# Loading v in two transfers a batch, reordering K's columns on their way out of PSUM, and setting the order of all work by a list scheduler inside a windowed-attention and adapter kernel

## The chip, the cores and the metric

The kernel runs on one core of a Trainium2 chip. The metric is the device time of one execution in microseconds, lower is better. A core has five engines that run their own instruction streams and wait for each other by semaphores: PE (TensorE, matrix products, with weight loads shown as PEld), DVE (VectorE), ACT (ScalarE), POOL (GpSimd) and SP (SyncE). Here POOL issues all loads, because they convert from float32 to float16 on the way, and SP issues all stores. Both run on the same DMA engines.

## The reference

Eight batches of eight heads, 576 positions, head size 64. Each position attends to positions at most 32 away. The result, laid out as 4608 rows of 512, goes through a mixture of eight adapters of rank 16, two per row, and is added to itself.

```python
scores = scale * np.matmul(q, k.transpose(0, 1, 3, 2))
mask = np.abs(pos[:, None] - pos[None, :]) <= window      # window = 32
scores = np.where(mask, scores, -1000000000.0)
attn = softmax(scores)
x = (attn @ v).transpose(0, 2, 1, 3).reshape(B * S, H * D)
logits = x @ w_gate                                       # 8 experts, the best 2 kept
w = softmax(the 2 kept logits)
out = x + sum over the 2 experts of w * ((x @ A[e]) @ B[e])
```

## The kernel before

Heads are taken in pairs (the index o is the half, n the pair within the batch, four pairs a batch), so that a unit u = 4b + n is one pair of one batch, 32 units in all. A unit has nine key blocks of 64 positions; eight consecutive blocks, of one unit or two, make a score tile, and there are 36 of them. The stages:

- **Loads.** `load` (line 85) brings q or k of a batch in three transfers of 96 partitions. `load_v` (93) brings v of a batch in eight transfers, two halves times four, each to 8 partitions, in rows of two positions. They land in one of three buffers `vbd`. `shift_v` (103) then copies, for each half, the second position of each row into 32 partitions further down, on DVE.
- **q and k to columns.** `regroup` (111) puts a tile of 96 rows into transposable order on DVE. `transposes` (181) does eight transposes for q and eight for k on PE into a PSUM tile of the pool `pt` (two buffers). q goes to `qT` by one ACT copy (192). k goes to `kT` in two copies of 64 partitions, the first half on DVE (204), the second on ACT (206). Within a block of 64 the k columns stand in the order (j, f), which is the order in which the eight v transfers place the positions.
- **Scores.** `score` (208): two matmuls write the mask into a PSUM tile of the pool `pw` (three buffers), eight add q times k, and one ACT instruction (222) takes the exponential into one of four `PT` buffers.
- **Values.** `pv` (226): 13 matmuls (238) with v and a column of ones, then a reciprocal (246) and a multiplication (247) on DVE into x.
- **Adapters**, once a batch, in four steps (`moe_step`, 325): five groups of four transposes of x (258), each with its DVE copy (261); 20 matmuls for router and first factor (269); the gate, twelve small DVE instructions and one on ACT (279 to 293); transposes back (302) and an ACT copy (305); output products (313, and 316 which adds x itself), in PSUM two groups at a time, an ACT copy (319) and stores on SP (323).

The order of work is written out by hand. Before the loop, the loads of batches 0 and 1 are issued on POOL, DVE clears the buffers of batch 0, and POOL clears those of the other batches (lines 164 to 166, by `zero` on line 135) and then issues six weight loads (170 to 179). In the loop over u, at the first unit of a batch come the loads of the batch after next; then regroup and transposes of one tile of the next batch, the scores for the next unit, the values of this unit, and one adapter step of the previous batch. The framework adds the semaphores, and each engine works its own stream off in order. It gives each load on POOL one of eight semaphores in turn, so the ninth waits for the first to land. A pool with n buffers makes the n+1st allocation wait until the first one is free.

Of the kernel before, what the change touches and what calls it, by code (L numbers as in the profile page):

```python
# [9 lines left out]
F16 = mybir.dt.float16  # L10
# [4 lines left out]


# [5 lines left out]

@with_exitstack
def kernel(
# [11 lines left out]
    B, H, S, D = q.shape  # L41
    assert (B, H, S, D) == (8, 8, 576, 64)
    N, DD = out.shape
    E = moe_w_gate.shape[1]
    R = moe_A.shape[2]
    ER = E * R
    NP = H // 2
    NB = 9
    NG = 5
    TB = 8  # L50
    J = 8
    PH = S // J
    NF = NP * PH
    NT3 = 3
    FT = NF // NT3
    GS = 188
    VD = D + 1
    V0 = 8
    VW = 136
    NS = NP * NB  # L60
    NEG = -30000.0
    NU = B * NP
    NT = NU * NB // TB
    QP = 32

    const = tc.alloc_tile_pool(name="const", bufs=1)
    load_pool = tc.alloc_tile_pool(name="load", bufs=2)
    cast_pool = tc.alloc_tile_pool(name="cast", bufs=2)
    x_pool = tc.alloc_tile_pool(name="xsb", bufs=2)
    moe_pool = tc.alloc_tile_pool(name="moe", bufs=2)  # L70
    ob_pool = tc.alloc_tile_pool(name="ob", bufs=3)
    small = tc.alloc_tile_pool(name="small", bufs=3)
    pw = tc.alloc_tile_pool(name="pw", bufs=3, space=bass.MemoryType.PSUM)
    pt = tc.alloc_tile_pool(name="pt", bufs=2, space=bass.MemoryType.PSUM)

    NV = 3
    vbd = [const.tile([128, NS, 2 * VW], F16, name=f"vbd{i}") for i in range(NV)]
    qTs = [const.tile([128, QP + NP * S + QP], F16, name=f"qT{i}") for i in range(2)]
    kTs = [const.tile([128, NS, 128], F16, name=f"kT{i}") for i in range(2)]
    NPT = 4  # L80
    PTs = [const.tile([128, TB, 256], F16, name=f"PT{i}") for i in range(NPT)]

    raw, qk = {}, {}

    def load(b, w):
        d = load_pool.tile([FT, NT3, 2, J * D], F16, tag=f"l{w}", name=f"l{w}")
        src = (q, k)[w][b].rearrange("(o n) (p j) d -> (n p) o (j d)", o=2, j=J)
        for t in range(NT3):
            nc.gpsimd.dma_start(out=d[:, t], in_=src[FT * t:FT * t + FT])  # L89
        raw[b, w] = d  # L90
        qk[b, w] = cast_pool.tile([FT, NT3, J, 2, D], F16, tag=f"c{w}", name=f"c{w}")

    def load_v(b):
        d = vbd[b % NV]
        src = v[b].rearrange("(o n) (a p j two) d -> o j p (n a) (two d)",
                             o=2, p=8, j=4, two=2)
        for o in range(2):
            for j in range(4):
                p0 = 64 * o + 8 * j
                c0 = VW * o + V0  # L100
                nc.gpsimd.dma_start(out=d[p0:p0 + 8, :, c0:c0 + 2 * D], in_=src[o, j])  # L101

    def shift_v(b):
        d = vbd[b % NV]
        for o in range(2):
            p0 = 64 * o
            c0 = VW * o + V0
            nc.vector.tensor_copy(out=d[p0 + 32:p0 + 64, :, c0:c0 + D],  # L108
                                  in_=d[p0:p0 + 32, :, c0 + D:c0 + 2 * D])

    def regroup(b, t):
        for w in (0, 1):
            nc.vector.tensor_copy(  # L113
                out=qk[b, w][:, t],
                in_=raw[b, w][:, t].rearrange("p o (j d) -> p j o d", j=J))

    load(0, 0)
    load(0, 1)
    load_v(0)

    ident = const.tile([128, 128], F16)
    make_identity(nc, ident)


    maskT = const.tile([128, 2, 2, 4, 8], F16)
    nc.gpsimd.memset(maskT, 0.0)
    nc.gpsimd.affine_select(out=maskT, in_=maskT, compare_op=ALU.is_ge, fill=NEG,
                            base=0, channel_multiplier=1,
                            pattern=[[0, 2], [-1, 2], [-2, 4], [-8, 8]])
    nc.gpsimd.affine_select(out=maskT, in_=maskT, compare_op=ALU.is_ge, fill=NEG,  # L130
                            base=64, channel_multiplier=-1,
                            pattern=[[0, 2], [1, 2], [2, 4], [8, 8]])

    def zero(eng, ap):
        eng.memset(ap, 0.0)  # L135

    def init_kq(i, eng):
        zero(eng, kTs[i][0:64, :, 64:128])
        zero(eng, kTs[i][64:128, :, 0:64])
        zero(eng, qTs[i][:, 0:QP])  # L140
        zero(eng, qTs[i][:, QP + NP * S:])

    def init_v(i, eng):
        zero(eng, vbd[i][0:64, :, VW + V0 - 1:VW + V0 + D])
        zero(eng, vbd[i][64:128, :, V0 - 1:V0 + D])
        eng.memset(vbd[i][0:64, :, V0 - 1:V0], 1.0)
        eng.memset(vbd[i][64:128, :, VW + V0 - 1:VW + V0], 1.0)

    init_kq(0, nc.vector)
    zero(nc.vector, PTs[0][:, :, 0:64])  # L150
    zero(nc.vector, PTs[0][:, :, 192:256])
    zero(nc.vector, qTs[0][:, QP + S:QP + S + 32])
    for t in range(NT3):
        regroup(0, t)
    for i in range(1, NPT):
        zero(nc.vector, PTs[i][:, :, 0:64])
        zero(nc.vector, PTs[i][:, :, 192:256])
    init_v(0, nc.vector)

    load(1, 0)  # L160
    load(1, 1)
    load_v(1)
    shift_v(0)
    init_kq(1, nc.gpsimd)
    init_v(1, nc.gpsimd)
    init_v(2, nc.gpsimd)

    WA_sb = const.tile([128, 4, ER + E], F16)
    for c in range(4):
        nc.gpsimd.dma_start(  # L170
            out=WA_sb[:, c, 0:ER],
            in_=moe_A.transpose([1, 0, 2])[128 * c:128 * c + 128],
        )
    nc.gpsimd.dma_start(
        out=WA_sb[:, :, ER:],
        in_=moe_w_gate.rearrange("(c p) e -> p c e", p=128),
    )
    B_sb = const.tile([128, DD], F16)
    nc.gpsimd.dma_start(out=B_sb, in_=moe_B.rearrange("e r d -> (e r) d"))

    def transposes(b, t):
        for w in (0, 1):
            src = qk[b, w].rearrange("p t j o d -> p t j (o d)")
            tp = pt.tile([128, 1024], F16, tag="t", name="tp")
            for j in range(J):
                slot = j if w == 0 else 4 * (j % 2) + j // 2
                nc.tensor.matmul(  # L187
                    out=tp[:, FT * slot:FT * slot + FT], lhsT=src[:, t, j, :],
                    rhs=ident[0:FT, 0:FT], is_transpose=True, start=True, stop=True)
            if w == 0:  # L190
                c0 = QP + J * FT * t
                nc.scalar.copy(  # L192
                    out=qTs[b % 2][:, c0:c0 + J * FT].rearrange("p (f j) -> p f j", j=J),
                    in_=tp[:, 0:J * FT].rearrange("p (j f) -> p f j", j=J))
            else:
                kt = tp[:, 0:J * FT].rearrange("p (j a f) -> p a j f", j=J, f=8)
                a0 = NS // NT3 * t
                a1 = a0 + NS // NT3
                for o in range(2):
                    dst = kTs[b % 2][64 * o:64 * o + 64, a0:a1, 64 * o:64 * o + 64]  # L200
                    dst = dst.rearrange("p a (j f) -> p a j f", f=8)
                    src_ = kt[64 * o:64 * o + 64]
                    if o == 0:
                        nc.vector.tensor_copy(out=dst, in_=src_)  # L204
                    else:
                        nc.scalar.copy(out=dst, in_=src_)  # L206

    def score(t):
        ps = pw.tile([128, TB, 128], F32, tag="w", name="ps")
        for i in range(0, TB, 4):  # L210
            nc.tensor.matmul(out=ps[:, i:i + 4],  # L211
                             lhsT=maskT.rearrange("p o a j f -> p (o a j f)"),
                             rhs=bcast(ident, 1, 4), start=True, stop=False)
        for i in range(TB):
            u, a = divmod(TB * t + i, NB)
            b, n = divmod(u, NP)
            c0 = S * n + 64 * a
            nc.tensor.matmul(  # L218
                out=ps[:, i], lhsT=kTs[b % 2][:, NB * n + a, :],
                rhs=qTs[b % 2][:, c0:c0 + 128],  # L220
                start=False, stop=(i % 4 == 3))
        nc.scalar.activation(out=PTs[t % NPT][:, :, 64:192], in_=ps,  # L222
                             func=AF.Exp, scale=1.0 / float(D) ** 0.5)

    xs = {}

    def pv(u):
        b, n = divmod(u, NP)
        if n == 0:
            xs[b] = x_pool.tile([128, NG, DD], F16, tag="x", name="xb")  # L230
        po = pw.tile([128, 1024], F32, tag="w", name="po")
# [174 lines left out]
```

## Time and profile before

| | us |
|---|---|
| time, median of 3 runs | 226.85 |
| lowest and highest run | 225.37, 232.73 |
| the profiled execution, its own time | 226.42 |
| its span, first to last instruction | 224.3 |
| busy: PE, DVE, ACT, POOL | 142.0, 122.5, 102.4, 98.9 |
| mean granted clock of TensorE | 0.888 |

The profile is one execution. Its page lists busy time by engine, then the span in 40 slices of 5.6 us with a digit for the busy share of each (9 is 90% or more; PEclk is the granted clock in tenths), the DMA queues, and the chain of waits: from the last instruction back, at each step to what released it. Groups of instructions are shown as line, engine, operation, output <- input, shape, count, then busy us, mean ns of one, then idle time of the engine before them and what ended it. In the timeline a row is start, duration, engine, line, operation. Matmuls overlap, so a PE row's duration is longer than its share of the engine, and the distance between two starts is the better price.

### The profile page before, as it was taken

The numbers are of one execution on the slowest core, as the hardware profiler recorded it, in microseconds if no ns is written. First come the engines' busy times: TensorE is split into PE (matmuls) and PEld (weight loads), VectorE is DVE, ScalarE is ACT, GpSimd is POOL, SyncE is SP. The second block draws the span as 40 slices with busy tenths as digits, with TensorE's granted clock in tenths as the row PEclk, the third lists the DMA queues.
The fourth block names the chain that finished last, engine by engine and source line by source line (L and its number), as shares of the span: only waits on it lengthen the run. The fifth ranks groups of instructions, "written<-read, shape, count | busy, mean of one in ns | idle before, by whom it ended". The sixth has DMA issues, their size and how long they took to land.

```text
span 224.3 us, 4265 instructions
## 1 busy us (share of the span) xinstructions
PE 142.0 (63%) x1720; PEld 114.2 (51%) x1720; DVE 122.5 (55%) x305; ACT 102.4 (46%) x125; POOL 98.9 (44%) x139
## 2 busy tenths in 40 slices
PE   0071995115769584968497759774977599639470
PEld 0041973115748473747375646563756476527440
DVE  5289469315532974395525962785258616743710
ACT  2012796011448445741667258626672576026032
POOL 8899799995776756097105930730000000000000
PEclk9998599955879999796969999999699969997967
DMA  6999910999999999899925995790230023002306
GB/s 74 167 108 193 91 5 1 29 154 145 122 177 157 256 147 154 178 179 77 189 85 133 101 165 136 158 79 1 85 129 3 0 82 130 3 3 82 129 0 210
DMA packets 57970, 24.20 MB, mean 108 GB/s; under 512 B 44000, under 2 KB 53344, under 8 KB 57952
## 3 DMA queue, kind: packets, MB, share of 16 engines
q0 software_dynamic: 52704, 14.51, 85.2%
q1 hardware_dynamic: 5248, 9.44, 12.0%
q8 instruction: 13, 0.21, 0.5%
q14 instruction: 5, 0.04, 0.1%
HBM read 28.85 MB, written 9.44 MB: 171 GB/s over the span
## 4 chain that ended last, share of the span: by engine, by line
PE 33%; DVE 25%; POOL 14%; DMA 14%; issue 7%; ACT 5%; ACTq 0%; DVEq 0%; POOLq 0%
DMA l<-in_k_dram 9%; PE pz L269 5%; PE po L238 5%; PE tx L258 5%; POOL l L89 5%; PE ps L211 5%; DVE xb L247 4%; DVE vbd L108 4%; DVE c L113 4%; POOL vbd L135 4%; PE ps L218 4%; PE pd L313 4%; PE pd L316 3%; DMA vbd<-in_v_dram 3%; DVE zs L293 3%
## 5 line engine op out<-in xcount | busy, mean ns | idle before, releaser
L101 POOL DMA_DIRECT2D vbd<-in_v_dram x64 | 47.4, 747 | 40.3 <-PE po L238 30.3
L187 PE MATMUL tp<-ident,c 96*128 96x96 f16 x384 | 27.8, 228 | 29.8 <-POOL ident masks.py:199 12.8
L222 ACT ACTIVATE PT<-ps 128x1024 f16<-128x1024 f32 x36 | 36.4, 1024 | 13.9 <-PE ps L218 13.6
L187 PEld LDWEIGHTS <-c 96*128 96x128 f16 x384 | 23.3, 111 | 33.7 <-DVE c L113 19.6
L192 ACT COPY qT<-tp 128x768 f16<-128x768 f16 x24 | 19.2, 799 | 44.3 <-PE tp L187 44.3
L238 PE MATMUL po<-vbd,PT 128*128 128x130 f16 x416 | 32.3, 227 | 11.0 <-DVE vbd L108 7.2
L238 PEld LDWEIGHTS <-PT 128*128 128x128 f16 x416 | 27.1, 102 | 13.0 <-DVE vbd L108 8.1
L113 DVE COPY c<-l 96x1024 f16<-96x1024 f16 x48 | 20.3, 456 | 15.3 <-DMA l<-in_q_dram 9.3
L206 ACT COPY kT<-tp 64x768 f16<-64x768 f16 x24 | 19.0, 793 | 20.7 <-DVE kT L204 20.6
L319 ACT COPY obt<-pd 128x1024 f32<-128x1024 f32 (+1 forms) x24 | 20.8, 870 | 14.2 <-PE pd L316 11.7
L211 PE MATMUL ps<-ident,maskT 128*128 128x512 f16 x72 | 27.0, 448 | 0.2
L218 PEld LDWEIGHTS <-kT 128*128 128x128 f16 x288 | 22.5, 110 | 8.5 <-issue 3.3
L247 DVE TENSOR_TENSOR xb<-po,rc 128x640 f16<-128x640 f32 x32 | 26.3, 823 | 0.9
L218 PE MATMUL ps<-qT,kT 128*128 128x128 f16 x288 | 26.5, 242 | 0.0
L204 DVE COPY kT<-tp 64x768 f16<-64x768 f16 x24 | 13.1, 546 | 24.1 <-PE tp L187 24.1
L246 DVE RECIPROCAL rc<-po 128x10 f32<-128x10 f32 x32 | 6.8, 213 | 31.4 <-PE po L238 31.3
L258 PE MATMUL tx<-ident,xb 128*128 128x128 f16 x160 | 16.9, 235 | 9.4 <-DVE xT L261 8.7
L313 PE MATMUL pd<-B_sb,zT 128*128 128x512 f16 x40 | 16.9, 422 | 4.2 <-ACT zT L305 4.2
L258 PEld LDWEIGHTS <-xb 128*128 128x128 f16 x160 | 12.6, 106 | 12.5 <-issue 10.4
L261 DVE COPY xT<-tx 128x512 f16<-128x512 f16 x40 | 16.4, 421 | 4.3 <-PE tx L258 2.3
L302 PE MATMUL tz<-ident,zs 128*128 128x128 f16 x40 | 3.6, 221 | 22.5 <-DVE zs L293 22.5
L316 PE MATMUL pd<-ident,xT 128*128 128x128 f16 x160 | 17.8, 242 | 0.0
(47 smaller groups left out, 163.4 us busy)
## 6 DMA issues: line engine op xcount, KB each, us to landing
out_dram<-obt SPq DMA_DIRECT2D x24, 256.0 KB, 2.4
l<-in_q_dram POOLq DMA_DIRECT2D x24, 192.0 KB, 5.4
l<-in_k_dram POOLq DMA_DIRECT2D x24, 192.0 KB, 6.3
vbd<-in_v_dram POOLq DMA_DIRECT2D x64, 72.0 KB, 6.9
out_dram<-obt SPq DMA_DIRECT2D x16, 192.0 KB, 2.4
WA_sb<-in_moe_A_dram POOLq DMA_DIRECT2D x4, 32.0 KB, 3.1
B_sb<-in_moe_B_dram POOLq DMA_DIRECT2D x1, 128.0 KB, 3.1
WA_sb<-in_moe_w_gate_dram POOLq DMA_DIRECT2D x1, 8.0 KB, 2.8
```

The lines of the kernel that those rows point to most:

```text
L101: nc.gpsimd.dma_start(out=d[p0:p0 + 8, :, c0:c0 + 2 * D], in_=src[o, j])
L113: nc.vector.tensor_copy(out=qk[b, w][:, t], in_=raw[b, w][:, t].rearrange("p o (j d) -> p j o d", j=J))
L187: nc.tensor.matmul(out=tp[:, FT * slot:FT * slot + FT], lhsT=src[:, t, j, :], rhs=ident[0:FT, 0:FT], is_transpose=True, start=True, stop=True)
L211: nc.tensor.matmul(out=ps[:, i:i + 4], lhsT=maskT.rearrange("p o a j f -> p (o a j f)"), rhs=bcast(ident, 1, 4), start=True, stop=False)
L218: nc.tensor.matmul(out=ps[:, i], lhsT=kTs[b % 2][:, NB * n + a, :], rhs=qTs[b % 2][:, c0:c0 + 128], start=False, stop=(i % 4 == 3))
L222: nc.scalar.activation(out=PTs[t % NPT][:, :, 64:192], in_=ps, func=AF.Exp, scale=1.0 / float(D) ** 0.5)
L238: nc.tensor.matmul(out=po[:, GS * g:GS * g + 2 * VD], lhsT=PTs[t % NPT][:, sl, off:off + 128], rhs=rhs[:, :, V0 - 1:V0 + D], start=(i == 0 ...
L247: nc.vector.tensor_tensor(out=xs[b].rearrange("p g (h n d) -> p g h n d", h=2, n=NP)[:, :, :, n], in0=pog[:, :, :, 1:VD], in1=bcast(rc, 3, ...
L258: nc.tensor.matmul(out=tp[:, 128 * c:128 * c + 128], lhsT=xs[b][:, g, 128 * c:128 * c + 128], rhs=ident, is_transpose=True, start=True, st ...
L313: nc.tensor.matmul(out=pd[:, i], lhsT=zT[:, g], rhs=B_sb, start=True, stop=False)
L316: nc.tensor.matmul(out=pd[:, i, 128 * c:128 * c + 128], lhsT=xT[:, g, c], rhs=ident, start=False, stop=(c == 3))
L319: nc.scalar.copy(out=ob[:, 0:n], in_=pd[:, 0:n])
```

## The change

Three things, and what goes with them.

**v in two transfers.** Each half of a batch's v comes as 32 partitions at once. Partition p of a half now holds positions 2p and 2p + 1 of its block, and the shift on DVE stays as it was.

```diff
-        src = v[b].rearrange("(o n) (a p j two) d -> o j p (n a) (two d)",
-                             o=2, p=8, j=4, two=2)
-        for o in range(2):
-            for j in range(4):
-                p0 = 64 * o + 8 * j
-                c0 = VW * o + V0
-                nc.gpsimd.dma_start(out=d[p0:p0 + 8, :, c0:c0 + 2 * D], in_=src[o, j])
+    def LV(b, o):
+        src = v[b, 4 * o:4 * o + 4].rearrange("n (a p two) d -> p (n a) (two d)", p=32, two=2)
+        p0, c0 = 64 * o, VW * o + V0
+        nc.gpsimd.dma_start(out=vbd[b % NV][p0:p0 + 32, :, c0:c0 + 2 * D], in_=src)
```

**K's columns in that order.** The copy from PSUM writes the order (r, f, j) in place of (j, f), and both halves are on ACT. The mask is built for the new order.

```diff
-                kt = tp[:, 0:J * FT].rearrange("p (j a f) -> p a j f", j=J, f=8)
...
-                    if o == 0:
-                        nc.vector.tensor_copy(out=dst, in_=src_)
-                    else:
-                        nc.scalar.copy(out=dst, in_=src_)
+        kt = ps("TR", b, 1, t)[:, 0:J * FT].rearrange("p (r j a f) -> p a r f j", r=2, j=4, f=8)
+        for o in range(2):
+            dst = kTs[b % 2][64 * o:64 * o + 64, BT * t:BT * t + BT, 64 * o:64 * o + 64]
+            nc.scalar.copy(out=dst.rearrange("p a (r f j) -> p a r f j", r=2, j=4),
+                           in_=kt[64 * o:64 * o + 64])
```

**A list scheduler.** The function `tasks` describes the kernel as tasks: loads LD and LV, shift SV, regroup RG, transposes TR, the copies EQ and EK, scores SC, exponential EX, values PV, their scaling MU, and the adapter steps TX, XE, PZ, G1, GA, G2, TZ, ZE, PD, OB and stores ST. Each has an engine, a cost, its predecessors, a due time (its unit number plus an offset of its kind) and, if it writes PSUM, the kind of buffer it takes and the task that gives it back. `plan` runs them through a model of the engines: the task that can start earliest goes next, and among those ready on an engine the one with the earliest due time. The kernel then emits all instructions in that order, and the PSUM buffer of each task is the one the model gave it.

```diff
+            lim = cand[0] + (horizon if e in ("PE", "ACT", "DVE") else 0.0)
...
+                if s <= lim and (pick is None or (t.due, t.seq) < (pick[1].due, pick[1].seq)):
+                    pick = (s, t)
+            if best is None or pick[0] < best[0]:
+                best = pick
...
+    ts, order = plan()
...
+    for t in order:
+        do[t.key[0]](*t.key[1:])
+        if t.key[0] in ("LD", "LV"):
+            loads += 1
+            if loads == 4:
+                constants()
+            elif loads == 8:
+                init_v(1, nc.gpsimd)
+            elif loads == 10:
+                init_kq(1, nc.gpsimd)
+            elif loads == 16:
+                weights()
+                init_v(2, nc.gpsimd)
```

What goes with it:

- The raw tiles of q and k lie in seven buffers each, by tile, in place of two by batch, and the regrouped ones in three by tile.
- The transposes of x go in three PSUM tiles of two, two and one groups, with one DVE copy for each tile.
- The third output copy of a batch (one group) is on DVE; the first two stay on ACT.
- POOL's clearing of buffers is spread between the loads, as the last lines of the diff show; identity and mask are made after the fourth load, and the weights are loaded after the sixteenth.
- The zeroing of `vbd` starts one column earlier, at an even column.
- PSUM has three wide and two narrow buffers as before.

In the built program PE has the same 1720 matmuls as before, and the loads come in the order q, k, q, k, half of v, q, k, half of v for each batch. On ACT, three q copies, six half copies of k and two exponentials (the first ahead of the last two half copies) come ahead of anything of batch 1.

More of the change, by code (lines that the diff above doesn't have):

```diff
@@ L14 @@
 AX = mybir.AxisListType
+B, H, S, D = 8, 8, 576, 64
+E, R, DD = 8, 16, 512
+ER = E * R
+NP = H // 2
+NB = 9
+NG = 5
+TB = 8
+J = 8
+PH = S // J
+NF = NP * PH
+NT3 = 3
+FT = NF // NT3
+GS = 188
+VD = D + 1
+V0 = 8
+VW = 136
+NS = NP * NB
+BT = NS // NT3
+NEG = -30000.0
+NU = B * NP
+NT = NU * NB // TB
+QP = 32
+NV, NPT, NRAW, NCAST, NX, NXT, NOB = 3, 4, 7, 3, 2, 2, 3
+NW, NTP = 3, 2
 def bcast(ap, axis, n):
@@ L111, in regroup @@
[L111 to L129, printed above, removed]
@@ L208, in score, with many @@
-    def score(t):
-        ps = pw.tile([128, TB, 128], F32, tag="w", name="ps")
+    assert tuple(q.shape) == (B, H, S, D)
+    const = tc.alloc_tile_pool(name="const", bufs=1)
+    psum = tc.alloc_tile_pool(name="psum", bufs=1, space=bass.MemoryType.PSUM)
+    small = tc.alloc_tile_pool(name="small", bufs=3)
+    def many(n, shape, dt, name):
+        return [const.tile(shape, dt, name=f"{name}{i}") for i in range(n)]
+    vbd = many(NV, [128, NS, 2 * VW], F16, "vbd")
+    qTs = many(2, [128, QP + NP * S + QP], F16, "qT")
@@ L314, in moe_out, with PD @@
+    def PD(b, h):
+        pd = ps("PD", b, h).rearrange("p (i c) -> p i c", c=DD)
+        for i, g in enumerate(gs(h)):
+            nc.tensor.matmul(out=pd[:, i], lhsT=zTs[b % 2][:, g], rhs=B_sb,
                              start=True, stop=False)
             for c in range(4):
-                nc.tensor.matmul(out=pd[:, i, 128 * c:128 * c + 128], lhsT=xT[:, g, c],
-                                 rhs=ident, start=False, stop=(c == 3))
-        ob = ob_pool.tile([128, 2, DD], F32, tag="ob", name="obt")
@@ L319, in moe_out, with OB @@
-        nc.scalar.copy(out=ob[:, 0:n], in_=pd[:, 0:n])
-        for i, g in enumerate(gs):
+                nc.tensor.matmul(out=pd[:, i, 128 * c:128 * c + 128],
+                                 lhsT=xTs[b % NXT][:, g, c], rhs=ident,
+                                 start=False, stop=(c == 3))
+    def OB(b, h):
+        n = len(gs(h))
+        dst = obs[(3 * b + h) % NOB][:, 0:n]
+        src = ps("PD", b, h).rearrange("p (i c) -> p i c", c=DD)[:, 0:n]
+        if ts["OB", b, h].eng == "ACT":
+            nc.scalar.copy(out=dst, in_=src)
+        else:
+            nc.vector.tensor_copy(out=dst, in_=src)
@@ L371 @@
-    for m in range(NU - NP, NU):
-        moe_step(m)
-    for p in (pt, pw, small, ob_pool, moe_pool, x_pool, cast_pool, load_pool, const):
+            nc.sync.dma_start(out=out[r0 + lo:r0 + hi], in_=obs[(3 * b + h) % NOB][lo:hi, i])
+    do = dict(LD=LD, LV=LV, SV=SV, RG=RG, TR=TR, EQ=EQ, EK=EK, SC=SC, EX=EX, PV=PV, MU=MU,
+              TX=TX, XE=XE, PZ=PZ, G1=G1, GA=GA, G2=G2, TZ=TZ, ZE=ZE, PD=PD, OB=OB, ST=ST)
+    ident = const.tile([128, 128], F16, name="ident")
+    mask = const.tile([128, 2, 2, 32], F16, name="mask")
@@ new lines, with constants @@
+    maskT = mask.rearrange("p o r c -> p (o r c)")
+    WA_sb = const.tile([128, 4, ER + E], F16, name="WA_sb")
+    B_sb = const.tile([128, DD], F16, name="B_sb")
+    def constants():
+        make_identity(nc, ident)
+        nc.gpsimd.memset(mask, 0.0)
+        nc.gpsimd.affine_select(out=mask, in_=mask, compare_op=ALU.is_ge, fill=NEG,
+                                base=0, channel_multiplier=1,
+                                pattern=[[0, 2], [-1, 2], [-2, 32]])
+        nc.gpsimd.affine_select(out=mask, in_=mask, compare_op=ALU.is_ge, fill=NEG,
+                                base=64, channel_multiplier=-1,
+                                pattern=[[0, 2], [1, 2], [2, 32]])
@@ new lines, in weights @@
+    def weights():
+        for c in range(4):
+            nc.gpsimd.dma_start(out=WA_sb[:, c, 0:ER],
+                                in_=moe_A.transpose([1, 0, 2])[128 * c:128 * c + 128])
+        nc.gpsimd.dma_start(out=WA_sb[:, :, ER:],
+                            in_=moe_w_gate.rearrange("(c p) e -> p c e", p=128))
+        nc.gpsimd.dma_start(out=B_sb, in_=moe_B.rearrange("e r d -> (e r) d"))
+    loads = 0
+    init_kq(0, nc.vector)
+    init_p(0, nc.vector)
+    nc.vector.memset(qTs[0][:, QP + S * 1:QP + S * 1 + 32], 0.0)
```

492 lines of the change are left out of this document (277 added, 215 removed).

## The prediction

> **What bounds the kernel now.** I read the page's first two parts first, for how full each engine is and where.
>
> ```profile
> span 224.3 us, 4265 instructions
> PE 142.0 (63%) x1720; PEld 114.2 (51%) x1720; DVE 122.5 (55%) x305; ACT 102.4 (46%) x125; POOL 98.9 (44%) x139
> ...
> PE   0071995115769584968497759774977599639470
> ...
> PEclk9998599955879999796969999999699969997967
> ...
> q0 software_dynamic: 52704, 14.51, 85.2%
> ```
>
> No engine is full: the busiest, PE, works 63% of the span. PE's digits show two holes at the start (slices 0 and 1, slices 7 and 8) and then a wave of some four slices, high and low. So the end is set by waits between engines. The chain of waits says the same.
>
> ```profile
> PE 33%; DVE 25%; POOL 14%; DMA 14%; issue 7%; ACT 5%; ACTq 0%; DVEq 0%; POOLq 0%
> ...
> 24.59 2.04 POOL kT L135
> ...
> 44.31 2.46 POOL l L89 x4
> ...
> 142.44 0.75 DVE vbd L108
> ...
> 165.88 0.75 DVE vbd L108
> ```
>
> The chain changes engine all the time. Its early part runs through POOL, which clears buffers from 24.59 and issues the next loads only at 44.31. Later the same step (the shift of v, line 108) comes round after 165.88 - 142.44 = 23.4 us: that is the period of one batch. The windows give the hole and one period:
>
> ```profile
> 40.00:48.00 8.00, 0.17 (x3) 0.00 (x0) 1.25 (x3) 0.00 (x0) 8.00 (x12) 0.77 1.33 71
> 48.00:72.00 24.00, 16.84 (x187) 14.09 (x188) 10.39 (x30) 10.60 (x14) 16.63 (x26) 0.72 1.86 149
> 165.00:188.00 23.00, 16.94 (x216) 13.57 (x214) 13.96 (x37) 12.65 (x17) 0.00 (x0) 0.93 0.14 47
> ```
>
> Columns: window, length, busy time of PE, weight load, DVE, ACT and POOL, granted clock, DMA share, GB/s. Between 40 and 48 only POOL works: the queue that issues loads has been clearing buffers, and everybody waits for batch 2. From 165 to 188 the DMA is nearly idle (0.14) and the batch still takes 23 us, though no engine has over 17: there the written order of the instructions binds. The list of waits adds one more:
>
> ```profile
> POOL vbd L101 <- PE po L238: 30.3, 3, 13.1
> ```
>
> POOL's 30 us are three waits for a free v buffer, with later loads queued behind them.
>
> **The change part by part.** These rows carry the prices (instruction and shape, count, busy time, mean ns):
>
> ```profile
> L192 ACT COPY qT<-tp 128x768 f16<-128x768 f16 x24 | 19.2, 799 | 44.3 <-PE tp L187 44.3
> L206 ACT COPY kT<-tp 64x768 f16<-64x768 f16 x24 | 19.0, 793 | 20.7 <-DVE kT L204 20.6
> L204 DVE COPY kT<-tp 64x768 f16<-64x768 f16 x24 | 13.1, 546 | 24.1 <-PE tp L187 24.1
> L261 DVE COPY xT<-tx 128x512 f16<-128x512 f16 x40 | 16.4, 421 | 4.3 <-PE tx L258 2.3
> L319 ACT COPY obt<-pd 128x512 f32<-128x512 f32 x8 | 4.7, 586 | 0.8 <-PE pd L316 0.2
> L135 DVE MEMSET vbd<- 64x2340 f16 x2 | 4.0, 2008 | 1.0 <-issue 0.5 <-DMA vbd<-in_v_dram 0.4
> L135 DVE MEMSET kT<- 64x1152 uint32 x2 | 2.0, 1018 | 1.3 <-PEq L390 1.0 <-issue 0.3
> L222 ACT ACTIVATE PT<-ps 128x1024 f16<-128x1024 f32 x36 | 36.4, 1024 | 13.9 <-PE ps L218 13.6
> L113 DVE COPY c<-l 96x1024 f16<-96x1024 f16 x48 | 20.3, 456 | 15.3 <-DMA l<-in_q_dram 9.3 <-DMA l<-in_k_dram 5.9
> ```
>
> *K order.* Both halves of k now leave PSUM on ACT with a read whose innermost step is 96 elements. The q copy reads that way today at 799 ns, the k copy without it takes 793: the stride is free. So ACT gains 24 x 0.793 = 19.0 us, and DVE loses 13.1. The third output copy goes from ACT (-4.7) to DVE; no row has it there, the bounds are 0.42 us (512 elements of f16, line 261) and twice that, 0.84, for elements twice as wide, and ACT's 0.59 for the same work lies between: I take 0.6, 8 x 0.6 = 4.8. The result's transposes leave in pairs: from 512 elements at 421 ns and 768 at 546, 1024 should take 0.67, so 16 x 0.67 + 8 x 0.42 = 14.1 against 16.4. The zeroing of v's first buffer starts one column earlier, an even one, and can run on words as the kT zeroing does: 2 x 1.05 against 4.0. Sums: ACT 102.4 + 19.0 - 4.7 = 116.7, or 14.6 a batch. DVE 122.5 - 13.1 + 4.8 - 2.3 - 1.9 = 110.0, less some 6.6 at the start, so 12.9 a batch.
>
> *PE* keeps its 1720 matmuls. What they cost back to back is read from start to start in the timeline:
>
> ```profile
> 150.44 0.84 PE L187 MATMUL tp<-ident,c 96*128 96x96 f16 x16
> 151.12 0.38 PE L211 MATMUL ps<-ident,maskT 128*128 128x512 f16 x1
> ...
> 161.63 0.38 PE L313 MATMUL pd<-B_sb,zT 128*128 128x512 f16 x1
> ...
> 162.07 0.59 PE L211 MATMUL ps<-ident,maskT 128*128 128x512 f16 x2
> 162.50 0.61 PE L218 MATMUL ps<-qT,kT 128*128 128x128 f16 x8
> 162.95 0.59 PE L211 MATMUL ps<-ident,maskT 128*128 128x512 f16 x2
> ...
> 163.83 0.91 PE L238 MATMUL po<-vbd,PT 128*128 128x130 f16 x13
> 164.58 0.38 PE L313 MATMUL pd<-B_sb,zT 128*128 128x512 f16 x1
> ```
>
> Eight transposes take 0.34, a score tile 0.88, a PV 0.75, an output group 0.44 (161.63 to 162.07), and a 128-column matmul 0.45/8 = 0.056. A batch: 6 x 0.34 + 4.5 x 0.88 + 4 x 0.75 + 5 x 0.44 + 45 x 0.056 (the other transposes and the router) = 13.7 us at full clock. At the span's mean clock, 0.888 (the PEclk digits), it is 15.5. So PE at 15.5 stands just above ACT at 14.6.
>
> [...]
>
> *v in two transfers.* The queue issues 16 in place of 64.
>
> ```profile
> L101 POOL DMA_DIRECT2D vbd<-in_v_dram x64 | 47.4, 747 | 40.3 <-PE po L238 30.3 <-DMA l<-in_k_dram 6.6 <-DMA l<-in_q_dram 2.2
> L89 POOL DMA_DIRECT2D l<-in_k_dram x24 | 15.1, 638 | 4.2 <-DMA vbd<-in_v_dram 1.9 <-DVE xT L261 0.8 <-DVE gate L291 0.4
> L170 POOL DMA_DIRECT2D WA_sb<-in_moe_A_dram x4 | 3.5, 903 | 0.0
> DMA to landing us min/median/max: 3.8/6.9/9.6
> ```
>
> One issue covers 32 x 36 = 1152 rows, where today it is 288 at 0.75 us. The nearest row by size is line 170, 128 x 8 = 1024 rows at 0.90; the upper bound is four of today's, 3.0. I take 1.0: 16 us in place of 47, none of it on the path, as POOL has slack either way (at 3.0 it is 48, as now). The rows moved stay the same, so the DMA keeps its work: q0's 85.2% of the span is 191 us of engine time, which at the 1.86 of window 48:72, where stores are few, is 103 us for all loads.
>
> *The order.* Loads run up to seven tiles ahead and POOL clears its buffers between them, so the hole at 40 to 48 should go. POOL's list up to batch 2 is 12 x 0.64 + 4 x 1.0 + the six weight loads and three clearings that today fill 24.6 to 44.3, some 33 us. Batch 2 is needed first at about 35 to 40, so this cover is thin.
>
> The start: DVE's clearing ends at about 8.5 (from the first row below, 4.1; plus 2.1 for v, 1.6 for the six PT halves by the second row, and gaps). Two regroups (0.46 each) and the transposes lead to ACT at 10. ACT then does, in its new order, three q copies, six half copies of k and two exponentials ahead of the first PV: 3 x 0.80 + 6 x 0.79 + 2 x 1.02 = 9.2. First PV at about 19.3, today 27.3.
>
> ```profile
> 4.01 0.07 DVE L135 MEMSET qT<- 128x16 uint32 x1
> ...
> 11.54 1.64 DVE L135 MEMSET PT<- 128x256 uint32 x6
> ...
> 27.32 0.57 PE L238 MATMUL po<-vbd,PT 128*128 128x130 f16 x7
> 34.98 4.18 DVE L108 COPY vbd<-vbd 32x2304 f16<-32x2304 f16 x2
> 205.62 0.91 PE L238 MATMUL po<-vbd,PT 128*128 128x130 f16 x13
> ```
>
> The tail today is 224.3 - 206.5 = 17.8 us after the last PV, a chain of single steps. The paired copies and the output copy on DVE save about 1 us; output products of batches 5 and 6 that now stand in the tail's PE stream cost up to 2. I take 17.5.
>
> [...] At 34.98 two shifts took 4.18 us beside POOL's clearings, against 0.75 later: 1.3 us more each. [...] By it the four shifts of the first two batches, which now run beside the clearings, give 5.3 us, and the end would be 164; I add none, as DVE has 12.9 us of work in a period of 15.5.
>
> *The sum.* From the first to the last PV lie 31 of 32 units, 7.75 batches: 19.3 + 7.75 x 15.5 + 17.5 = 156.9. The profiled execution lasted 226.42 for a span of 224.3, so 2.1 comes on top: 159 us. It lies 0.2% under the median of the runs, which I don't correct.
>
> **The rivals.**
> - *The clock stays up, ACT binds.* Period 14.6: 19.3 + 113 + 17.5 + 2.1 = 152. For it: full digits of PEclk in busy stretches. Against: window 165:188 has PE at 74% and still 0.93.
> - *The DMA feeds too slowly.* It must move all loads before the last batch. At 1.86 that takes q0's 103 us; if waits for buffers hold it at 1.45, it is 132, from 1.3 on, and then four PVs at some 2.5 each and the tail: 1.3 + 132 + 10 + 17.5 + 2.1 = 163, and 173 at a rate of 1.34. For: only eight transfers are ever out. Against: each v transfer now holds four times as much.
> - *Dependencies still bind.* The PSUM buffers stay three and two, and a real order that slips waits in line on each engine. At a period of 20 (23.4 now) the time is 194. For: today's 23 us with DMA idle. Against: the new streams put other batches' work between a producer and its user.
> - *v's long transfers bind, and it is slower.* The place is the wait of the shift of v, in front of PV. If rows of one transfer go as serially as now, four times 6.9 us is 27.6 for one and 55 for a batch. Past a period of 25 us, when two in a row need over 12.5 each, the time passes 232. Against: 6.9 is mostly queueing behind seven others, and the two overlap. [...]
> - *The reordering does nothing*, as the end was set by latency along one chain: 222 to 231.
>
> **How the numbers follow.** Forecast 159 with chance 0.46; clock up 0.22; slow DMA 0.13; dependencies 0.13; slower 0.04; nothing 0.02. The range goes from 147 (period 14.0: PE at full clock, and a last batch that has no copies of q and k to make) to 180 (period 18.2, PE's busy time as counted, 142 / 8 = 17.8, and a little). That holds the first three; 0.19 lies outside. A difference of 2% is about what runs of this kernel can tell, as they spread from 225.4 to 232.7: faster 0.94, same 0.02, slower 0.04.
>
> **What would show it.** Right: the first PV near 19; no window with only POOL busy; the shift of v every 15 to 16 us; ACT near 117 us and DVE near 110; line 101's successor at 1 us with 16 issues. Wrong: idle time of PE and DVE put down to loads (DMA rival); PE idle in each batch behind copies on ACT (dependencies); PEclk at 1.0 and ACT over 90% busy (clock); landing of v above 12 us (slower).

## The result and the profile after

The changed kernel took 199.88 us (median of 4 runs, 199.40 to 204.04) against 227.64 for the one before. The ratio is 0.880, with a 95% interval of 0.870 to 0.890. It is faster, as forecast, but by 28 us, where 68 were forecast, and outside the range. The medians here and below take in a few disturbed runs at a lower clock; ratios leave those out, and where a run below has none, too few undisturbed runs of the kernel before stood beside it.

The page of the changed kernel, its first three parts:

```profile
span 198.0 us, 4213 instructions
...
PE 137.4 (69%) x1720; PEld 110.5 (56%) x1720; DVE 114.2 (58%) x273; ACT 114.5 (58%) x141; POOL 65.7 (33%) x91
...
PE   0058395546688655695777979896789899789380
...
PEclk9999958585569999789999999999999999999955
...
DMA packets 38770, 24.12 MB, mean 122 GB/s; under 512 B 24800, under 2 KB 34144, under 8 KB 38752
...
q0 software_dynamic: 33504, 14.43, 64.9%
```

Nothing is full here either. PE's digits, after two empty slices, swing between 3 and 9 up to slice 19 (94 us); from there to the tail they are 6 to 9. The busy times of ACT and DVE are near the forecast (116.7 and 110), so the work is priced right and something else makes the engines wait. One number is not as forecast: the queue of the loads has 33,504 packets in place of 52,704, for nearly the same bytes (14.43 MB for 14.51).

The prices, from the groups of the changed kernel (line numbers are its own: 311 k's copies, 289 regroup, 369 the paired copies of x's transposes, 446 the output copy on DVE, 279 the load of v):

```profile
L311 ACT COPY kT<-T 64x768 f16<-64x768 f16 x48 | 38.1, 793 | 4.9 <-PE T L297 4.6
L289 DVE COPY c<-l 96x1024 f16<-96x1024 f16 x48 | 25.8, 573 | 0.3
L369 DVE COPY xT<-T 128x1024 f16<-128x1024 f16 x16 | 11.0, 691 | 29.1 <-PE T L363 18.1 <-PE W L323 7.0 <-ACT zT L426 3.3
L446 DVE COPY ob<-W 128x512 f32<-128x512 f32 x8 | 5.5, 686 | 7.9 <-PE W L435 7.1 <-DMA out_dram<-ob 0.8
L279 POOL DMA_DIRECT2D vbd<-in_v_dram x16 | 13.5, 845 | 25.4 <-PE W L341 23.2 <-DMA vbd<-in_v_dram 2.1
```

k's copy costs 793 ns with the strided read, the paired copy 0.69 (forecast 0.67), the output copy 0.69 (0.6), an issue of v 0.85 (1.0). Only the regroups are dearer, 573 ns in place of 456.

Where the time is lost shows when the three terms of the sum are read off. One row of the view of the tile `vbd` has the starts of the first and the last PV matmul:

```profile
L341 PE MATMUL W<-vbd,PT x416: 218/219/315, 26.3 to 177.7; 128*128 128x130 f16 x139
```

| term, us | forecast | changed kernel | the same, bound to the plan's order (run e1) |
|---|---|---|---|
| start to first PV | 19.3 | 26.3 | 22.7 |
| first to last PV (a batch: that / 7.75) | 120.1 (15.5) | 151.4 (19.5) | 113.8 (14.7) |
| last PV to end of span | 17.5 | 20.3 | 21.3 |
| outside the span, profiled execution | 2.1 | 2.0 | 1.8 |
| sum | 159.0 | 200.0 | 159.6 |

Of the 41 us missed, 31 are in the second term, the period of a batch times 7.75. That period is a mean of two stages. The first scaling of each batch (the reciprocal on DVE, line 350, every fourth of its 32 rows in the timeline) starts at these times:

| batch | 0 | 1 | 2 | 3 | 4 | 5 | 6 | 7 |
|---|---|---|---|---|---|---|---|---|
| changed kernel, us | 28.0 | 56.6 | 83.7 | 101.3 | 120.2 | 137.4 | 155.1 | 172.7 |
| run e1, us | 23.7 | 38.6 | 56.5 | 69.1 | 86.1 | 100.3 | 116.4 | 130.8 |

In the changed kernel batches 0 and 1 take 28.6 and 27.1 us and the five after them 17.8 each on average; in e1 it is 14.9 and 17.8, then 14.9. So of the 40 us between the two, 23 lie in the first two batches, 15 in the five after, and the rest in the start, less a tail that is slightly shorter. The streams of DVE, ACT and PE of the changed kernel show how the early stretch looks, each from its timeline:

```profile
8.80 4.81 DVE L289 COPY c<-l 96x1024 f16<-96x1024 f16 x4
...
17.12 2.54 DVE L284 COPY vbd<-vbd 32x2304 f16<-32x2304 f16 x1
28.01 0.22 DVE L350 RECIPROCAL rc<-W 128x10 f32<-128x10 f32 x1 [8.35 <-PE W L341]
...
31.01 0.82 DVE L351 TENSOR_TENSOR x<-W,rc 128x640 f16<-128x640 f32 x1
31.75 3.21 DVE L289 COPY c<-l 96x1024 f16<-96x1024 f16 x3
...
51.05 0.69 DVE L369 COPY xT<-T 128x1024 f16<-128x1024 f16 x1 [7.12 <-PE T L363]
53.12 1.02 DVE L369 COPY xT<-T 128x1024 f16<-128x1024 f16 x2 [1.38 <-PE T L363]
54.18 0.75 DVE L284 COPY vbd<-vbd 32x2304 f16<-32x2304 f16 x1
```

```profile
22.14 2.86 ACT L328 ACTIVATE PT<-W 128x1024 f16<-128x1024 f32 x3
34.93 0.80 ACT L303 COPY qT<-T 128x768 f16<-128x768 f16 x1 [9.93 <-PE T L297]
```

```profile
34.07 1.46 PE L297 MATMUL T<-ident,c 96*128 96x96 f16 x16 [1.59 <-DVE c L289]
...
54.98 2.98 PE L341 MATMUL W<-vbd,PT 128*128 128x130 f16 x26 [1.33 <-DMA l<-in_k_dram]
```

The regroups of batch 1 (31.75) stand on DVE behind three scalings (28.01 to 31.83), and DVE has waited 8.35 us for PV before those. The regroups themselves wait for no load. So the transposes of batch 1 start at 34.07, and ACT is idle for 9.93 us. At 54.18 it happens again: the shift of v stands behind three copies of x's transposes, though its v was issued at 22.64 and such a load lands within 10.8 us in this run, and PV follows at 54.98 (the profile names a load of k as the releaser there, which PV does not read; the shift ends at 54.93). In the plan both steps come earlier. The order of the built program beside the plan's own (the latter from run e1, where it is enforced), from the fifth regroup on:

```
changed kernel, DVE                                plan, DVE
23 L289 TensorCopy c0_2_91<-l0_2_77 96x1024        23 L289 TensorCopy c0_2_91<-l0_2_77 96x1024
24 L289 TensorCopy c1_2_94<-l1_2_84 96x1024        24 L289 TensorCopy c1_2_94<-l1_2_84 96x1024
25 L284 TensorCopy vbd0_64<-vbd0_64 32x36x64       25 L284 TensorCopy vbd0_64<-vbd0_64 32x36x64
26 L350 Reciprocal rc_304<-W1_107 128x10           26 L289 TensorCopy c0_0_89<-l0_3_78 96x1024
27 L351 TensorTensor x0_95<-W1_107,rc_304          27 L289 TensorCopy c1_0_92<-l1_3_85 96x1024
28 L350 Reciprocal rc_338<-W2_108 128x10           28 L350 Reciprocal rc_304<-W1_107 128x10
29 L351 TensorTensor x0_95<-W2_108,rc_338          29 L351 TensorTensor x0_95<-W1_107,rc_304
30 L350 Reciprocal rc_350<-W1_107 128x10           30 L289 TensorCopy c0_1_90<-l0_4_79 96x1024
31 L351 TensorTensor x0_95<-W1_107,rc_350          31 L289 TensorCopy c1_1_93<-l1_4_86 96x1024
32 L289 TensorCopy c0_0_89<-l0_3_78 96x1024        32 L350 Reciprocal rc_338<-W2_108 128x10
```

The list scheduler only sets the order in which the kernel emits its instructions. The framework sorts them once more when it builds the streams. PE's stream is cut the same way: it has eight score matmuls, eight transposes, four score matmuls and eight transposes where the plan has whole score tiles, and the first three PV in one piece.

### The profile page after: what moved, and what is told of

It reads as the page before. It is cut to its first block, busy times and chain, and to the rows that moved or that the text cites. A ratio compares the mean times of both kernels' runs of the same rounds, so it can differ in the third digit from the quotient of the medians.

```text
span 198.0 us, 4213 instructions
## 1 busy us (share of the span) xinstructions
PE 137.4 (69%) x1720; PEld 110.5 (56%) x1720; DVE 114.2 (58%) x273; ACT 114.5 (58%) x141; POOL 65.7 (33%) x91
## 2 busy tenths in 40 slices
DMA packets 38770, 24.12 MB, mean 122 GB/s; under 512 B 24800, under 2 KB 34144, under 8 KB 38752
## 3 DMA queue, kind: packets, MB, share of 16 engines
q0 software_dynamic: 33504, 14.43, 64.9%
## 5 line engine op out<-in xcount | busy, mean ns | idle before, releaser
L328 ACT ACTIVATE PT<-W 128x1024 f16<-128x1024 f32 x36 | 36.1, 1025 | 12.5 <-PE W L323 10.6
L341 PE MATMUL W<-vbd,PT 128*128 128x130 f16 x416 | 33.9, 240 | 11.0 <-DVE vbd L284 6.0
L311 ACT COPY kT<-T 64x768 f16<-64x768 f16 x48 | 38.1, 793 | 4.9 <-PE T L297 4.6
L297 PE MATMUL T<-ident,c 96*128 96x96 f16 x384 | 25.6, 220 | 17.5 <-DVE c L289 15.1
L303 ACT COPY qT<-T 128x768 f16<-128x768 f16 x24 | 19.2, 799 | 30.6 <-PE T L297 27.7
L297 PEld LDWEIGHTS <-c 96*128 96x128 f16 x384 | 21.9, 106 | 24.4 <-DVE c L289 19.3
L323 PE MATMUL W<-qT,kT 128*128 128x128 f16 x288 | 25.4, 229 | 6.1 <-ACT kT L311 5.2
L317 PE MATMUL W<-ident,mask 128*128 128x512 f16 x72 | 24.2, 420 | 6.5 <-ACT PT L328 4.0
L351 DVE TENSOR_TENSOR x<-W,rc 128x640 f16<-128x640 f32 x32 | 26.2, 820 | 0.8
L279 POOL DMA_DIRECT2D vbd<-in_v_dram x16 | 13.5, 845 | 25.4 <-PE W L341 23.2
L435 PE MATMUL W<-ident,xT 128*128 128x128 f16 x160 | 17.3, 231 | 0.0
```

What stands on the lines that cost most here:

```text
L297: nc.tensor.matmul(out=tp[:, FT * slot:FT * slot + FT], lhsT=src[:, j, :], rhs=ident[0:FT, 0:FT], is_transpose=True, start=True, stop=True)
L303: nc.scalar.copy(out=qTs[b % 2][:, c0:c0 + J * FT].rearrange("p (f j) -> p f j", j=J), in_=ps("TR", b, 0, t)[:, 0:J * FT].rearrange("p (j ...
L311: nc.scalar.copy(out=dst.rearrange("p a (r f j) -> p a r f j", r=2, j=4), in_=kt[64 * o:64 * o + 64])
L317: nc.tensor.matmul(out=p[:, i:i + 4], lhsT=maskT, rhs=bcast(ident, 1, 4), start=True, stop=False)
L323: nc.tensor.matmul(out=p[:, i], lhsT=kTs[b % 2][:, NB * n + a, :], rhs=qTs[b % 2][:, c0:c0 + 128], start=False, stop=(i % 4 == 3))
L328: nc.scalar.activation(out=PTs[T % NPT][:, :, 64:192], in_=ps("SC", T).rearrange("p (i c) -> p i c", c=128), func=AF.Exp, scale=1.0 / floa ...
```

## The experiments

Three theories stood at first. A: the second sorting costs the time. B: POOL's clearing, beside DVE's copies and ahead of the loads, costs the first 60 us. C: the period is set by dependencies through the PSUM buffers in any order.

**The plan's order, bound (e1).** Each instruction of PE, ACT and DVE gets an edge that lets it issue only after the one before it in the plan. It is an edge of order, not a wait.

```diff
     for t in order:
+        n0 = len(nc.cur_bb.bb.instructions)
         do[t.key[0]](*t.key[1:])
+        pin(n0)
...
+    def pin(n0):
+        for ins in list(nc.cur_bb.bb.instructions)[n0:]:
+            if ins.engine not in pinned:
+                continue
+            if ins.engine in last:
+                tc.add_manual_dep(ins, last[ins.engine], mybir.DependencyInfo(
+                    mybir.DependencyClass.NoSync, mybir.DependencyReason.DATA), reason="plan")
+            last[ins.engine] = ins.name
```

> The changed kernel, with each instruction of PE, ACT and DVE bound to issue after the one that the plan puts before it, so that the streams are the plan's own. Theory A (the framework sorted the plan's order anew, and the new order puts steps behind steps they don't need, such as regroups of batch 1 behind three scalings of batch 0): 160 to 175 us, the last 25 units at 16 us a batch or less. Theory B (POOL's clearing, beside DVE's copies and ahead of the loads, costs the first 60 us): 190 to 200, the first PV still at 26. Theory C (the period is set by dependencies through three wide and two narrow PSUM buffers, in any order): 195 to 205.

159.92 us (159.23 to 160.91), ratio 0.706 to before, 0.692 to 0.720. The page, then DVE's timeline, then windows (length, PE, weight load, DVE, ACT, POOL, clock, DMA share, GB/s):

```profile
span 157.8 us, 4220 instructions
...
PE 122.1 (77%) x1720; PEld 102.7 (65%) x1720; DVE 118.0 (75%) x273; ACT 113.0 (72%) x141; POOL 66.2 (42%) x91
...
PEclk9999999999599999999999999999999999999567
```

```profile
19.69 0.84 DVE L289 COPY c<-l 96x1024 f16<-96x1024 f16 x2
23.74 0.22 DVE L350 RECIPROCAL rc<-W 128x10 f32<-128x10 f32 x1 [3.21 <-PE W L341]
...
32.88 1.63 DVE L284 COPY vbd<-vbd 32x2304 f16<-32x2304 f16 x1
34.53 0.69 DVE L369 COPY xT<-T 128x1024 f16<-128x1024 f16 x1
```

```profile
30.00:40.00 10.00, 5.34 (x82) 4.56 (x80) 6.80 (x9) 5.08 (x7) 9.89 (x12) 1.00 1.60 82
50.00:60.00 10.00, 10.00 (x162) 8.83 (x160) 8.04 (x20) 9.93 (x14) 4.82 (x8) 1.00 1.45 208
60.00:80.00 20.00, 17.45 (x264) 14.75 (x263) 17.54 (x47) 17.55 (x23) 9.83 (x14) 1.00 1.49 202
80.00:100.00 20.00, 19.25 (x292) 16.45 (x290) 16.11 (x40) 18.38 (x24) 7.84 (x12) 1.00 1.28 216
```

The regroups of batch 1 now come at 19.69, 12 us earlier, and the shift of v ahead of the copies of x. In these windows from 50 on PE is busy for 87 to 100% and ACT for 88 to 99%, at a granted clock of 1.00. The mean period is 113.8 / 7.75 = 14.7 us. With the same instructions, buffers and transfers the time falls by 40 us, so theory A is shown and C refuted.

**Loads first (e2, e3).** POOL issues all sixteen loads of batches 0 and 1 and only then clears buffers; e2 leaves the framework's sorting, e3 binds the plan's order too.

```diff
+    first = [t for t in order if t.key[0] in ("LD", "LV")][:16]
+    for t in first:
+        do[t.key[0]](*t.key[1:])
...
+    init_kq(1, nc.gpsimd)
+    init_v(1, nc.gpsimd)
+    weights()
+    init_v(2, nc.gpsimd)
```

> The changed kernel, with POOL issuing all loads of batches 0 and 1 before it clears the buffers of batches 1 and 2; the clearing and the weights then come in one piece. Theory A (order sorted anew): 193 to 200. Theory B (POOL's clearing in the early part): first regroups at 0.42 us each, first PV at 19 to 21, batch 1 regrouped by 25, and 180 to 188 us. Theory C (buffers): 193 to 200, with any early gain lost later.

> The changed kernel with both: the plan's own order on PE, ACT and DVE, and all loads of batches 0 and 1 ahead of POOL's clearing. Theory A: as e1, within 5 us. Theory B: as e2, within 5 us. A and B together: 150 to 160 us, near the forecast of 159. Theory C: above 190.

e2: 191.45 us (187.06 to 191.63). e3: 161.98 (161.12 to 162.37). DVE's timeline and the PV row of e3:

```profile
8.81 1.49 DVE L289 COPY c<-l 96x1024 f16<-96x1024 f16 x4
...
15.97 4.66 DVE L289 COPY c<-l 96x1024 f16<-96x1024 f16 x2 [0.34 <-DMA l<-in_q_dram]
```

```profile
L341 PE MATMUL W<-vbd,PT x416: 217/219/315, 19.9 to 138.8; 128*128 128x130 f16 x139
```

The first four regroups take 1.49 us without POOL's clearing beside them and 4.81 with it, and the first PV comes at 19.9, as the forecast has it. But the clearing now meets the next regroups (4.66 us for two), and the end is no earlier than in e1. In e2 the first regroups take 1.40 us, but the first PV comes at 23.1 and batch 1 is regrouped only by 31, so B's signs are met in part. So B is real at its place. It moves the end by 8 us by the medians, and by 13 us by e2's profiled execution of 187.06, only where the order is the framework's; with the plan's order it is made up or paid later. e2 also brings the loads of batch 1 forward, and it does not tell these two parts of B apart.

**v and k alone, order by hand (e4).** The kernel before, with v in two transfers and k's columns and mask as in the change; k's halves stay on DVE and ACT.

```diff
-            for j in range(4):
...
-                nc.gpsimd.dma_start(out=d[p0:p0 + 8, :, c0:c0 + 2 * D], in_=src[o, j])
+            src = v[b, 4 * o:4 * o + 4].rearrange("n (a p two) d -> p (n a) (two d)", p=32, two=2)
...
+            nc.gpsimd.dma_start(out=d[p0:p0 + 32, :, c0:c0 + 2 * D], in_=src)
...
-                kt = tp[:, 0:J * FT].rearrange("p (j a f) -> p a j f", j=J, f=8)
+                kt = tp[:, 0:J * FT].rearrange("p (r j a f) -> p a r f j", r=2, j=4, f=8)
```

> The kernel before, with v in two transfers a batch and k's columns and mask in the new order, and nothing else: k's halves stay on DVE and ACT, the order of work stays written by hand. If the gain comes from the order of work alone: 222 to 229 us, as before, POOL's issue time down by 33 us and off the path. If the transfers of v matter (fewer places in the queue of eight, landing as early as now or earlier): 210 to 220.

208.36 us (206.81 to 210.46), ratio 0.917, 0.900 to 0.934. That is a little below the 210 to 220 expected if v's transfers matter. The two small parts gain 19 of the 28 us of the change by themselves, and the rest of the change, the scheduler as built above all, adds the other 8. On DVE the strided read is not free; the row of k's first half, before 546 ns:

```profile
L201 DVE COPY kT<-tp 64x768 f16<-64x768 f16 x24 | 22.7, 945 | 21.2 <-PE tp L184 21.0
```

**Which stream (e5).** e1 with one engine bound at a time, one changed word each:

```diff
-    pinned = list(eng_of.values())
+    pinned = [eng_of["DVE"]]
```

> The changed kernel with the plan's order bound on DVE alone; PE and ACT stay as the framework sorts them. If the sorting of one engine makes the loss, this is the likeliest one, as the first regroups of batch 1 stand behind three scalings there: 165 to 180 us. If the loss is in all three streams together, since a step that is late on one engine waits on the next one's order: 185 to 200.

> The changed kernel with the plan's order bound on PE alone. If PE's stream makes the loss (it stands idle most often behind other engines' results): 165 to 180 us. If all three streams count together: 180 to 200.

> The changed kernel with the plan's order bound on ACT alone. ACT has the most work in a batch, so if its stream makes the loss: 165 to 180 us. If all three streams count together: 190 to 202.

DVE alone 182.73 us, PE alone 175.04, ACT alone 197.34 (two runs each, within 3 us). PE's stream holds the largest part of the loss, 25 of 40 us; DVE's 17, ACT's 3. I had named DVE the likeliest, and its 182.73 lies between its two expected ranges. The three add to 45, a little more than 40, which fits that repairing one stream mends part of what another spoils.

**Order by hand, bound (e6).** e4 with the same `pin` over its loop.

> The kernel before with v in two transfers and k's columns in the new order, its order of work by hand and bound on PE, ACT and DVE as in the run with the plan's order. If binding an order is what helps, whichever order it is: 160 to 180 us. If it is the plan's order that helps and binding only lets it through: 205 to 225, since by hand all of an adapter step stands ahead of the next scores.

216.71 us (214.19 to 218.33), ratio 0.955, 0.947 to 0.963: slower than the 208 of e4. Binding is no gain in itself. The framework's sorting helps the order by hand by 8 us and spoils the plan by 40.

**How many partitions (e7, e8).** e1 with v again in eight transfers of 8 partitions, and in four of 16.

```diff
-        nc.gpsimd.dma_start(out=vbd[b % NV][p0:p0 + 32, :, c0:c0 + 2 * D], in_=src)
+        for i in range(0, 32, 8):
+            p0 = 64 * o + i
+            nc.gpsimd.dma_start(out=vbd[b % NV][p0:p0 + 8, :, c0:c0 + 2 * D], in_=src[i:i + 8])
```

> The run with the plan's order bound, with v again in eight transfers a batch of 8 partitions, the new column order kept. If the number of partitions sets how many packets the DMA makes of the same bytes: packets back from 38.8 to about 58 thousand, the loads' engine time from 80.8% of 158 us, 128 us, back to about 190, and a time of 175 to 195 us. If only the order of work counts: 158 to 165 us.

> The run with the plan's order bound, with v in four transfers a batch of 16 partitions. If packets double only where a transfer has fewer than 16 partitions: 38.8 thousand packets and 158 to 166 us, a few us for two more places in the queue of eight. If packets or cost follow the size of a transfer in steps: about 45 thousand packets and 165 to 180 us.

174.26 us (172.30 to 175.54) with 8 partitions, 164.35 (163.95 to 166.94) with 16, against 159.92 with 32. With 8 that is just under the expected 175 to 195, and with 16 within 158 to 166. The packet lines and the line of the loads' queue, 8 partitions first, then 16, then the queue with 32 (e1):

```profile
DMA packets 57971, 24.21 MB, mean 140 GB/s; under 512 B 44000, under 2 KB 53344, under 8 KB 57952
...
q0 software_dynamic: 52704, 14.51, 117.1%
```

```profile
DMA packets 39027, 24.13 MB, mean 146 GB/s; under 512 B 25056, under 2 KB 34400, under 8 KB 39008
...
q0 software_dynamic: 33760, 14.43, 106.5%
```

```profile
q0 software_dynamic: 33504, 14.43, 80.8%
```

Transfers of 8 partitions made half as many packets again, of nearly the same bytes; 16 and 32 did not. The engine time of the queue (its share times the span) does not follow the packets: it is 117.1% of 173.2, 203 us, with 8 partitions, 176 with 16 and 128 with 32. Of the 14 us that v's two transfers are worth here, 10 lie between 8 and 16 partitions and 4 between 16 and 32. Packets, engine time and the number of transfers change together in the first step, the last two in the second, so which of them costs the time is not shown.

**Clearing later (e9, e10).** e1 with the third v buffer cleared behind the loads of batch 2 (e9), and besides with the second q and k buffers cleared behind four loads of batch 1 and the second v buffer behind eight (e10).

```diff
-            elif loads == 8:
-                init_v(1, nc.gpsimd)
-            elif loads == 10:
+            elif loads == 12:
                 init_kq(1, nc.gpsimd)
             elif loads == 16:
                 weights()
+                init_v(1, nc.gpsimd)
+            elif loads == 24:
                 init_v(2, nc.gpsimd)
```

> The run with the plan's order bound, with POOL's clearing of the third v buffer moved behind the loads of batch 2. Theory D (the hole from 30 to 40 in that run, PE 5.3 of 10 us, comes from batch 2's loads being issued only at 34.8, behind this clearing): loads of batch 2 at about 29.5, and 153 to 157 us. If the hole has another cause: 158 to 162.

> As the run before this one, and POOL's clearing of the second k and v buffers later too, behind four and eight loads of batch 1. If clearing beside the first regroups (4.81 us for four where 1.7 would do) delays the end: first PV at 20 to 21 in place of 22.7, and 151 to 155 us. If the early delay is made up later, as it was when all loads came first: within 2 us of the run before this one.

e9: 160.62 us (159.91 to 162.45), no gain. Batch 2's loads are issued at 30.39 in place of 34.80, and from 30 to 40 of its profiled execution (162.45 us) PE is busy 7.18 us in place of 5.34. So the hole is smaller, and the end does not move. But the clearing now stands ahead of batch 3's loads, which go out at 42.44 in place of 40.27, so the run does not tell what earlier loads alone are worth: theory D is neither shown nor refuted by it. e10: 156.95 (156.59 to 159.98), the fastest of all, 3 us below e1. Its own theory was not put to the test, since POOL's clearing of the second k buffers still runs beside the first regroups. The rows are DVE's regroups, then POOL's clearing:

```profile
8.81 6.66 DVE L289 COPY c<-l 96x1024 f16<-96x1024 f16 x4
```

```profile
10.53 2.04 POOL L475 MEMSET kT<- 64x2304 f16 x1
12.62 2.18 POOL L476 MEMSET kT<- 64x2304 f16 x1
```

The row of PV and the window 30 to 40:

```profile
L341 PE MATMUL W<-vbd,PT x416: 218/219/232, 23.3 to 133.7; 128*128 128x130 f16 x139
...
30.00:40.00 10.00, 8.19 (x128) 6.93 (x126) 8.69 (x16) 7.08 (x9) 9.85 (x11) 1.00 1.35 172
```

The first regroups are slower, 6.66 us for 4.81, and the first PV comes at 23.3. The gain is in the mean period, 110.4 / 7.75 = 14.2 us, and there in the first two batches alone: they take 29.1 us in place of e1's 32.7, from the first scaling of batch 0 (24.30) to that of batch 2 (53.42), and the five after them 14.9 each, as in e1. Batch 2's loads go out at 28.43 and batch 3's at 39.73, neither later than in e1, and PE is busy 8.19 us from 30 to 40. That fits theory D, but e10 moves three clearings at once, so it is not shown.

## Why the prediction was wrong, by its own steps

**The step that failed is "the order".** The prediction took the streams to hold the plan, and put a chance of 0.46 on a period of 15.5 us from PE's price at the mean clock. The sum's term 7.75 x 15.5 = 120.1 rests on that step, and it measured 151.4. The rival "dependencies still bind" got 0.13, with "the new streams put other batches' work between a producer and its user" against it. That rival came nearest: it gave a period of 20 and 194 us, measured are 19.5 and 200. Its waiting in line on each engine is what the runs show; its PSUM buffers are not, since e1 has the same ones. That its number fits is in part luck: 19.5 is the mean of two batches at 28 and later ones at 17.8. What I set against it holds for the plan, and the built program has another order. The page of before could not show it; the order of the built program could, but the forecast rests there on the order of the loads and on ACT's first steps, where the two nearly agree (in the trace of the changed kernel four exponentials stand ahead of the first copy of batch 1, not two, and in the plan three). Bound to the plan, the kernel takes 159.92 us, where the forecast said 159. That match is luck in part too: in e1 the start is 3.4 us and the tail 3.8 us longer than forecast, and the time between them 6.3 us shorter.

**The three terms.** The period was the error in the changed kernel, 151.4 us for 120.1. In e1 it is 14.7, close to ACT's 14.6 and below the 15.5 at the old mean clock. The granted clock was 0.888 before, with PE busy for 63% of the span, 0.896 in the changed kernel with 69%, and 0.962 in e1 with 77%; e1's digits of PEclk are 9 from the start to the tail but for one slice. So once the order holds, the rival "the clock stays up, ACT binds" has the period right and the clock too; that ACT binds is not shown, as from 80 to 100 PE is busy for 96% and ACT for 92%. The start was 7 us late, for two reasons. In the built stream half of a fifth score tile, which waits 2.26 us for a PSUM buffer, stands ahead of the first PV; the plan's order (e1) brings it from 26.3 to 22.7. And the first regroups are slowed by POOL's clearing; without that (e3) it is 19.9. The tail was 3 to 4 us longer than the 17.5 taken, in e1, e3 and e10 too; that term was undersized, and why was not tested.

**DVE beside POOL's clearing.** I added nothing for the regroups and shifts beside POOL's clearing, as DVE had slack. The first four regroups took 4.81 us beside it in the changed kernel, and 1.49 without it in e3. Counted at the 1.3 us more that each shift took beside the clearings before (4.18 us for two, 0.75 for one later), four shifts put the end 5 us later by my estimate. e2, which also has earlier loads, gained 8 to 13 with the order as sorted, e3 nothing with the plan's, so what it costs at the end depends on the order.

**The transfers.** "The rows moved stay the same, so the DMA keeps its work" was wrong. Packets fell from 57,970 to 38,770, and the queue's engine time from 191 us to 64.9% of 198, 128. I took v's transfers to be off the path on POOL's issue time alone. They are worth 14 us in e1's order (e7). In the order by hand v and k together gave 19, and k's part there costs DVE time, so the gain is v's by inference; v alone was not run. With 8, 16 and 32 partitions the queue's engine time is 203, 176 and 128 us for the same rows, so the step counted rows where the shape of the transfers matters. The rival of long transfers that bind had its price from a landing time of 6.9 us for a quarter; whole ones landed in a median of 8.1.

**The prices** were right: ACT 114.5 for 116.7, DVE 114.2 for 110.0 (the regroups make it up), v's issue 0.85 for 1.0, paired and output copies within 0.1.

## What to carry to other kernels

Before forecasting from an order that a kernel sets, compare the built stream of each engine with it, all the way: the same instructions took 200 and 160 us. A framework's sorting can help an order by hand and spoil a planned one, so bind the order where a plan is meant to hold, and measure both. Try fewer transfers of more partitions for the same bytes, even where issue time is off the path: with one order, v in 32 partitions took 160 us, in 16 164 and in 8 174. Before calling a mean a period, read the batches one by one: here the first two lost more than the five after them.

## What the runs showed of the hardware

With v in loads of 8 partitions, converted on the way, the whole kernel made 57,971 packets (e7), with 16 it made 39,027 (e8) and with 32 38,771 (e1). The engine time of the loads' queue was 203, 176 and 128 us in the same runs. k's copy out of PSUM, with an innermost step of 96 elements, took DVE 945 ns (e4) in place of 546 (before), and ACT 794 (e4) in place of 793 (before). Four regroups on DVE took 4.81 us beside a clearing on POOL (the changed kernel) and 1.49 without it (e3).
